# Linear attention with a mixture-of-depths expert on one core: when the expert's weights, the decayed keys and the first batch's slots come in the order of work

## The chip, the cores and the metric

The kernel runs on one core of a Trainium2 chip. The metric is the device time of one execution in microseconds; lower is better. Before the change it is 191.12 us, the median of three runs (190.85 to 191.2).

## What is computed

The inputs are q, k and v with 4 batches, 8 heads, 768 positions and a head dimension of 64, in fp32, and one decay factor per head. The reference first computes a causal linear attention with decay, in blocks of 64 positions:

```python
for b in range(nb):
    intra = (q_b k_b^T * Dmask) v_b              # inside the block, Dmask = lam ** (i - j)
    inter = (q_b * lam_pow) kv_state             # from all blocks before
    out_b = intra + inter
    kv_state = lam_block * kv_state + (k_b * rev_pow)^T v_b
```

The heads are then laid side by side, so that x has 4 batches of 768 rows of 512 values. For each batch a score `x @ w_gate` is computed for every row, the 128 rows with the highest scores are chosen, and for these alone `x + sigmoid(score) * (relu(x @ w1) @ w2)` replaces the row. w1 is 512 x 1024 and w2 is 1024 x 512. All other rows are the attention's output.

## The kernel before, in words

The work is cut into 24 groups of 128 rows (two blocks of 64), six groups to a batch. The loop at L601 goes through the groups; pass g is called step g. Every engine executes its instructions in the order in which the program issues them, so the order of the calls in the loop body is the schedule. The tile framework adds the waits that the data and the buffers need.

Step g does these things for different groups, in this order:

- `load(g + 6)` issues the three input DMAs (q, k, v; 256 KB each, rows of 64 values) on SP's queue, L68. There are seven buffers of each input.
- `load_weights(g - 4)` issues one of eight weight DMAs of 512 KB in steps 4 to 11, on the same queue: four for w1 (L84), four for w2 (L87).
- `decay_state(2g + 4)`, GpSimd (POOL) at L263, multiplies a state by its decay.
- `keys_decayed(g + 3)`, POOL at L183, multiplies the keys by their powers of the decay; it gives kd, which `state_products(g + 3)` needs in the next step.
- `from_scores(g)` (L295) and `outputs(g)` finish group g: TensorE (PE) multiplies, ScalarE (ACT) copies the result to x_b (L309, L311) and stores it (L321).
- `scores(g + 1)` (L230), `from_states(g + 1)` (L284) and `masked(g + 1)` (L237, VectorE, DVE) start group g + 1. `from_states` needs qs, the decayed queries.
- `state_products(g + 2)` (L253) multiplies decayed keys and values into pu, two PSUM banks of which there is one set. It can overwrite them only when `next_state` of the group before has read them.
- `transposes(g + 2)` (L195, L206) with ACT's copies to qT and kT (L198, L212), `queries_decayed(g + 2)` (POOL, L217, gives qs), `next_state(2g + 4)` (DVE, L274), `decay_state(2g + 5)`.
- `gate_scores(g)` (DVE, L334) computes the scores of group g. It needs wg_b, the gate weights repeated on all 128 partitions.
- `row(g - 1)` (L357 on PE, L360 on ACT, L363 on DVE), then `next_state(2g + 5)`, then `compare(g - 1)` (L373) count, for each row, how many scores beat it. At the first row group of a batch `row` also zeroes the counters "beaten" on POOL (L352).

When a batch is complete, `plan(b)` spreads its expert over later steps. `ranks` (L409, L414) turns the counts into ranks and a matrix of hits, `tokens` (L425 to L434) turns the hits into row numbers, `fetch` (L448) gathers the rows xs from the output in memory, `gate` (L458 to L473) transposes them and computes the sigmoid, and sixteen pieces do the two matrix products: eight `hidden` pieces (ph, L486) and eight `back` pieces (py, L500), the last of which also adds the residual (L508) and scatters the rows back (L512). The calls that `plan` puts into a step run with `in_order(pieces)`.

For the first batch (b = 0, s = 6) ranks come in step 7, tokens and fetch in step 8, the gate in step 9 behind `state_products(11)`, and the pieces in steps 9 to 14 as 2, 3, 3, 3, 3, 2. For b = 1 (s = 12) ranks, tokens and fetch are all in step 13, and for b = 2 in step 19. The third batch has one piece in each of steps 21 to 23, and the rest at the end together with the fourth batch's expert.

Of the kernel before, what the change touches and what calls it, by code (L numbers as in the profile page):

```python
# [8 lines left out]
FP32 = mybir.dt.float32  # L9
# [8 lines left out]
def kernel(  # L18
# [12 lines left out]
    nc = tc.nc  # L31

    B, H, S, D = q.shape
    HD = H * D
# [3 lines left out]
    C = 64  # L38
    NT = S // L
    NHP = H // 2  # L40
    NDC = HD // 128
    NFC = F // 128
    NGR = (CAP + 127) // 128
    NG = B * NT
# [5 lines left out]
    const = ctx.enter_context(tc.tile_pool(name="const", bufs=1))  # L50
# [4 lines left out]
    ps_o = ctx.enter_context(tc.tile_pool(name="ps_o", bufs=2, space=PSUM))  # L55
# [6 lines left out]
    def load(g):  # L62
        b, c = divmod(g, NT)
        rows = slice(c * L, (c + 1) * L)
        tiles = []
        for name, src in (("qn", q), ("kn", k), ("vn", v)):
            t = ld.tile([128, H, D], FP32, name=name)
            nc.sync.dma_start(out=t[:], in_=src[b, :, rows, :].rearrange("h p d -> p h d"))  # L68
            tiles.append(t)
        loaded[g] = tiles  # L70


    lam_b = const.tile([128, H], FP32, name="lam_b")
    nc.scalar.dma_start(out=lam_b[:], in_=lam.unsqueeze(0).broadcast_to([128, H]))
    for g in range(3):
        load(g)
    wg_b = const.tile([128, HD], FP32, name="wg_b")
    nc.sync.dma_start(out=wg_b[:], in_=moe_w_gate.unsqueeze(0).broadcast_to([128, HD]))
    w1_sb = const.tile([128, NDC, F], FP32, name="w1_sb")
    w2_sb = const.tile([128, NFC, HD], FP32, name="w2_sb")  # L80

    def load_weights(i):
        if i < NDC:
            nc.sync.dma_start(out=w1_sb[:, i, :], in_=moe_w1[i * 128 : (i + 1) * 128, :])  # L84
        else:
            j = 2 * (i - NDC)
            nc.sync.dma_start(  # L87
                out=w2_sb[:, j : j + 2, :],
                in_=moe_w2[j * 128 : (j + 2) * 128, :].rearrange("(c p) e -> p c e", p=128),
            )  # L90
# [12 lines left out]
        out=not_before[:], in_=not_before[:], compare_op=ALU.is_ge, fill=0.0,  # L103
# [13 lines left out]
    if CAP % 128:  # L117
# [4 lines left out]
            out=in_cap[:], in_=in_cap[:], compare_op=ALU.is_gt, fill=0.0,  # L122
# [5 lines left out]
    for hh in range(2):  # L128
        for hp in range(NHP):
            h = 2 * hp + hh  # L130
            nc.vector.tensor_tensor_scan(
                out=mask[:, hh, hp, :], data0=lam_b[:, h : h + 1].broadcast_to([128, C]),
# [12 lines left out]
    for hp in range(NHP):  # L145
        for c in range(2):
            nc.vector.tensor_tensor_scan(
                out=qpow[:, hp, c, :], data0=lam_p[:, hp : hp + 1].broadcast_to([128, C]),
# [27 lines left out]
    def quarters():  # L176
        for hp in range(NHP):
            for hh, c in ((0, 0), (1, 1), (1, 0), (0, 1)):
                yield hp, hh, c

    def keys_decayed(g):
        kd = att.tile([128, H, D], FP32, name="kd")
        nc.gpsimd.tensor_tensor(  # L183
            out=kd[:], in0=loaded[g][1][:],
            in1=kpow[:].rearrange("p a b -> p (a b)").unsqueeze(2).broadcast_to([128, H, D]),
            op=ALU.mult,
        )
        kds[g] = kd
# [35 lines left out]
    def scores(g):  # L224

        qT, kT = qTs.pop(g), kTs.pop(g)
        po = ps_o.tile([128, 2, 2, NHP, C], FP32, name="po")
        pos[g] = po
        for hp, hh, c in quarters():
            nc.tensor.matmul(  # L230
                po[half[c], hh, 1, hp, :], lhsT=kT[half[hh], hp, half[c]],
                rhs=qT[half[hh], hp, half[c]], start=True, stop=True, skip_group_check=True,
            )
# [10 lines left out]
    def start_u(g):  # L244
        us[g] = [ps_u.tile([128, 512], FP32, name=f"pu{c}") for c in range(2)]
# [125 lines left out]
    def count(b, t, cols, op, at):  # L371
        cmp = mod.tile([128, S], BF16, name="cmp")
        nc.vector.tensor_scalar(  # L373
            out=cmp[:, : cols.stop - cols.start], in0=rows_[b][:, cols],
            scalar1=scs[b][:, t : t + 1], scalar2=None, op0=op, op1=ALU.add,
            accum_out=beatens[b][:, t, at : at + 1],
        )

    def count_later(b, groups, last):
        for t in groups:  # L380
            if upto[b][t] < last:
                cols = slice((upto[b][t] + 1) * L, (last + 1) * L)
                count(b, t, cols, ALU.is_gt, last)
                upto[b][t] = last

    def compare(g):
        b, t = divmod(g, NT)
        first = upto[b].pop(NT + t, 0)
        count(b, t, slice(first * L, (t + 1) * L), ALU.is_ge, t)
        if t == NT // 2 - 1 or t == NT - 1 or (b == B - 1 and t == NT - 2):  # L390
            count_later(b, range(t), t)
        elif t == NT - 2:
            count_later(b, range(NT // 3), t)

    def compare_older(g):

        b, t = divmod(g, NT)
        if t > 0:
            count(b, t, slice(0, t * L), ALU.is_ge, 0)
            upto[b][NT + t] = t  # L400
# [119 lines left out]

    gates, later, ranked = {}, {}, {}
    busy_until = [0]

    def put(step, key, piece):
        later.setdefault(step, []).append((key, piece))
# [5 lines left out]
    def plan(b):  # L533
        last = b == B - 1
        s = (b + 1) * NT
        ranks, tokens = places(b)
        if last:

            def last_row():
                compare_older(NG - 1)  # L540
                row(NG - 1, us[NG][1])
                compare(NG - 1)
                ranks()

            put(s, 35, last_row)
            put(s, 85, tokens)
        else:
            ranked[s + 1] = ranks

            where = (s + 1, 25) if b > 0 else (s + 2, 5)  # L550
            put(*where, tokens)
        for i in range(NGR):
            s = max(s, busy_until[0])
            fetch, gate, pieces = expert(b, i)
            if s + 3 >= NG:
                s = max(s, NG)
                put(s, 86, fetch)
                put(s + 1, 0, gate)
                for j, piece in enumerate(pieces):
                    put(s + 2, j, piece)  # L560
                busy_until[0] = s + 3
                continue
            put(s + 1, 26, fetch) if i > 0 or b > 0 else put(s + 2, 6, fetch)
            gates[s + 3] = gate

            whole = s + 9 <= NG
            counts = [2, 3, 3, 3, 3, 2] if whole else [1, 1, 1]
            assert len(pieces) == 16
            where = [(s + 3 + i, 10 * (j + 1)) for i, n in enumerate(counts) for j in range(n)]
            where = [w for w in where if w[0] < NG]  # L570
            where += [(NG, 10 * (j + 1)) for j in range(len(pieces) - len(where))]
            for (step, key), piece in zip(where, pieces):
                put(step, key, piece)
            busy_until[0] = s + 6 if whole else NG
# [3 lines left out]
    queries_decayed(0)  # L578
    keys_decayed(1)
    scores(0)  # L580
    start_u(0)
    state_products(0)
    next_state(0)
# [13 lines left out]
    decay_state(3)  # L597
    next_state(3)

    n_w = NDC + NFC // 2  # L600
    for g in range(NG):  # L601
        if g + AHEAD < NG:
            load(g + AHEAD)
        if 0 <= g - NT + 2 < n_w:
            load_weights(g - NT + 2)
        if g >= 2 * NT and kept:
            store_kept()
        if g + 2 < NG:
            decay_state(2 * g + 4)
        if g + 3 < NG:  # L610
            keys_decayed(g + 3)
        from_scores(g)
        outputs(g)
        if g + 1 < NG:
            scores(g + 1)
            from_states(g + 1)
            masked(g + 1)
        if g in ranked:
            ranked.pop(g)()
        if g % NT == 0 and g > 0 and NGR:  # L620
            compare_older(g - 1)
        if g + 2 <= NG:
            start_u(g + 2)
        if g + 2 < NG:
            state_products(g + 2)
        if g in gates:
            gates.pop(g)()
        if g + 2 < NG:
            transposes(g + 2)
            queries_decayed(g + 2)  # L630
            next_state(2 * g + 4)
            decay_state(2 * g + 5)
        gate_scores(g)
        pieces = later.pop(g, [])

        rows = [r for r in {NG - 2: [g - 1, g], NG - 1: []}.get(g, [g - 1]) if r >= 0 and NGR]
        if g % NT == 0:
            for r in rows:
                row(r)
        else:  # L640
            in_order(pieces)
            for r in rows:
                row(r, us[NG][0] if r == NG - 2 else None)
        if g + 2 < NG:
            next_state(2 * g + 5)
        for r in rows:
            compare(r)
        if g % NT == 0:
            in_order(pieces)
        if g % NT == NT - 1 and NGR:  # L650
            plan(g // NT)
# [35 lines left out]
```

## Time and profile before

| what | value |
|---|---|
| device time, median of three | 191.12 us |
| span of the profiled run | 184.5 us |
| PE busy | 149.4 us, 81% |
| POOL busy | 103.1 us, 56% |
| DVE busy | 110.7 us, 60% |
| ACT busy | 67.5 us, 37% |
| DMA on the input and weight queue | 23.34 MB in 76688 packets |

The page of a profile gives the busy time of each engine, the span in 40 slices with the busy share of each slice in tenths, the chain of waits that ended last, and the groups of instructions that cost most. In a timeline a row has the start, the duration, engine, line, operation, the tile written and the tile read, the number of instructions joined in the row, and in brackets the idle time of the engine before it with what ended the idle. "issue" is an engine's wait for which the profile shows no releaser. PE matmul rows count the records that the profile has; a matmul in fp32 leaves two records.

### The profile page before, as it was taken

Reading aid. Unit: us, or ns where it says so; the run is one execution under the profiler, and the core shown is the slowest. Engines: PE = TensorE matmul, PEld = TensorE weight load, DVE = VectorE, ACT = ScalarE, POOL = GpSimd, SP = SyncE. Lnnn points to the kernel's source line nnn. Section 1 sums busy time; section 2 is a strip of 40 time slices with the busy share of each in tenths; the row PEclk is TensorE's granted clock in tenths of the full one; section 3 lists DMA queues with packets and bytes.
Section 4 is the critical chain, followed back from the end, with each engine's and each line's share of the span. In section 5 each row is a group of like instructions: output and inputs, shape, how many; then the busy total and the mean of one; then the engine's idle time right before and its main releaser. Section 6 shows DMA issues by size and latency. Waiting matters only on the chain.

```text
span 184.5 us, 8089 instructions
## 1 busy us (share of the span) xinstructions
PE 149.4 (81%) x3520; PEld 121.1 (66%) x3520; DVE 110.7 (60%) x357; ACT 67.5 (37%) x185; POOL 103.1 (56%) x110
## 2 busy tenths in 40 slices
PE   0787577877665809999979999999989969989980
PEld 0675555766654709999566699995767869449630
DVE  2942455675998625665985678759967889430010
ACT  2223355553343504555234455453425631111100
POOL 4286878666785953375837866758678400220002
PEclk9999999999999996999999999999999999999996
DMA  4999999999999999999999979911121311011001
GB/s 102 226 221 245 231 242 225 226 228 234 206 221 246 272 292 260 255 226 240 327 349 265 282 210 250 213 47 62 60 62 59 117 57 60 0 57 57 0 0 57
DMA packets 80898, 32.23 MB, mean 175 GB/s; under 512 B 75616, under 2 KB 75616, under 8 KB 80864
## 3 DMA queue, kind: packets, MB, share of 16 engines
q1 hardware_dynamic: 76688, 23.34, 57.1%
q10 hardware_dynamic: 3536, 6.30, 9.4%
q0 software_dynamic: 640, 2.10, 3.4%
q8 instruction: 27, 0.44, 1.1%
q14 instruction: 7, 0.06, 0.1%
HBM read 24.38 MB, written 7.34 MB: 172 GB/s over the span
## 4 chain that ended last, share of the span: by engine, by line
PE 47%; issue 14%; POOL 10%; DMA 9%; DVE 8%; SPq 6%; ACT 4%; POOLq 1%; ACTq 0%; DVEq 0%
PE ph L486 11%; PE py L500 9%; PE tq L195 6%; SPq L68 5%; PE pu L253 5%; POOL qs L217 5%; PE po L284 4%; PE po L295 4%; POOL decayed L263 3%; ACT qT L198 3%; DMA kn<-in_k_dram 3%; PE po L230 3%; DMA xs<-out_dram,tok 3%; PE pu L206 2%; DVE state L274 2%
## 5 line engine op out<-in xcount | busy, mean ns | idle before, releaser
L263 POOL TENSOR_TENSOR decayed<-state,decay 128x256 f32<-128x256 f32 x40 | 36.7, 919 | 15.0 <-DVE state L274 13.2
L217 POOL TENSOR_TENSOR qs<-qT,qpow 128x512 f32<-128x512 f32 x24 | 31.4, 1307 | 24.4 <-ACT qT L198 22.9
L274 DVE TENSOR_TENSOR state<-pu,decayed 128x256 f32<-128x256 f32 x40 | 16.9, 422 | 25.6 <-ACT kT L212 17.1
L486 PE MATMUL ph<-xsT,w_sb 128*128 128x128 f32 x256 | 31.2, 278 | 0.7 <-ACT xsT L462 0.7
L198 ACT COPY qT<-tq 128x512 f32<-128x512 f32 x24 | 14.0, 584 | 45.4 <-PE tq L195 44.2
L486 PEld LDWEIGHTS ph<-xsT,w_sb 128*128 128x128 f32 x256 | 29.8, 193 | 1.2 <-ACT xsT L462 0.9
L500 PE MATMUL py<-w_sb,hs 128*128 128x512 f32 x64 | 29.7, 600 | 0.4 <-ACT qT L198 0.4
L373 DVE TENSOR_SCALAR_CACHE_REDUCE cmp<-sc_row,sc 128x128 bf16<-128x128 f32 (+3 forms) x66 | 29.9, 497 | 0.0
L183 POOL TENSOR_TENSOR kd<-kn,kpow 128x512 f32<-128x512 f32 x24 | 26.0, 1084 | 4.9 <-DVE kpow L137 3.3
L334 DVE CUSTOM_DVE_ANT_0 xg<-x_b,wg_b 128x512 f32<-128x512 f32 x24 | 25.6, 1066 | 0.0
L284 PE MATMUL po<-state,qs 64*64 64x64 f32 x704 | 18.4, 222 | 8.0 <-issue 4.3
L253 PE MATMUL pu<-vn,kd 64*64 64x64 f32 x704 | 19.3, 225 | 3.8 <-DVE state L274 3.7
L230 PE MATMUL po<-qT,kT 64*64 64x64 f32 x768 | 18.0, 226 | 4.5 <-issue 3.9
L284 PEld LDWEIGHTS po<-state,qs 64*64 64x64 f32 x704 | 14.9, 134 | 10.1 <-issue 5.2
L195 PE MATMUL tq<-ident,qn 128*128 128x128 f32 x96 | 16.9, 303 | 5.1 <-DMA qn<-in_q_dram 5.1
L253 PEld LDWEIGHTS pu<-vn,kd 64*64 64x64 f32 x704 | 16.2, 138 | 4.8 <-DVE state L274 4.5
L230 PEld LDWEIGHTS po<-qT,kT 64*64 64x64 f32 x768 | 14.9, 138 | 5.5 <-issue 4.5
L500 PEld LDWEIGHTS py<-w_sb,hs 128*128 128x128 f32 x64 | 11.3, 190 | 10.9 <-issue 9.8
L295 PEld LDWEIGHTS po<-vn,p 64*64 64x64 f32 x768 | 13.4, 134 | 6.8 <-issue 3.2
L311 ACT COPY x_b<-po 64x256 f32<-64x256 f32 x48 | 17.6, 367 | 0.6
L237 DVE TENSOR_TENSOR p<-po,mask 128x512 f32<-128x512 f32 x24 | 16.5, 686 | 1.8 <-PE po L284 1.7
L295 PE MATMUL po<-vn,p 64*64 64x64 f32 x768 | 16.7, 224 | 0.9 <-DVE p L237 0.9
(61 smaller groups left out, 148.1 us busy)
## 6 DMA issues: line engine op xcount, KB each, us to landing
qn<-in_q_dram SPq DMA_DIRECT2D x24, 256.0 KB, 5.6
kn<-in_k_dram SPq DMA_DIRECT2D x24, 256.0 KB, 5.9
vn<-in_v_dram SPq DMA_DIRECT2D x24, 256.0 KB, 5.8
out_dram<-x_b ACTq DMA_DIRECT2D x18, 256.0 KB, 3.3
w_sb<-in_moe_w_dram SPq DMA_DIRECT2D x8, 512.0 KB, 5.5
out_dram<-x_b ACTq DMA_DIRECT2D x2, 768.0 KB, 7.4
wg_b<-in_moe_w_gate_dram SPq DMA_DIRECT2D x1, 256.0 KB, 6.1
xs<-out_dram,tok POOLq DMA_INDIRECT x4, 4.4
```

The lines of the kernel that those rows point to most:

```text
L183: nc.gpsimd.tensor_tensor(out=kd[:], in0=loaded[g][1][:], in1=kpow[:].rearrange("p a b -> p (a b)").unsqueeze(2).broadcast_to([128, H, D]) ...
L195: nc.tensor.transpose(tq[:, hp, :], in_=loaded[g][0][:, 2 * hp : 2 * hp + 2, :], identity=ident[:])
L217: nc.gpsimd.tensor_tensor(out=qs[:], in0=qTs[g][:], in1=qpow[:].rearrange("p a c i -> p a (c i)"), op=ALU.mult)
L230: nc.tensor.matmul(po[half[c], hh, 1, hp, :], lhsT=kT[half[hh], hp, half[c]], rhs=qT[half[hh], hp, half[c]], start=True, stop=True, skip_g ...
L253: nc.tensor.matmul(us[g][c][half[hh], hp * D : (hp + 1) * D], lhsT=kd[half[c], h, :], rhs=vn[half[c], h, :], start=True, stop=True, skip_g ...
L263: nc.gpsimd.tensor_tensor(out=t[:], in0=states[n][:], in1=decay[:], op=ALU.mult)
L284: nc.tensor.matmul(pos[g][half[hh ^ c], hh, 0, hp, :], lhsT=qs[half[hh], hp, half[c]], rhs=states[n][half[hh], hp, :], start=(hp == 0), st ...
L295: nc.tensor.matmul(pos[g][half[hh ^ c], hh, 0, hp, :], lhsT=p[half[c], hh, hp, :], rhs=vn[half[c], 2 * hp + hh, :], start=(hp == 0 and (2 ...
L334: nc.vector.tensor_tensor_reduce(out=xg[:], in0=x_bs[b][:, t].rearrange("p a b e -> p (a b e)"), in1=wg_b[:], scale=1.0, scalar=0.0, op0=A ...
L373: nc.vector.tensor_scalar(out=cmp[:, : cols.stop - cols.start], in0=rows_[b][:, cols], scalar1=scs[b][:, t : t + 1], scalar2=None, op0=op, ...
L486: nc.tensor.matmul(ph[:, fc % 4, :], lhsT=w1_sb[:, dc, fc * 128 : (fc + 1) * 128], rhs=keep["xsT"][:, dc, :], start=(dc == 0), stop=(dc == ...
L500: nc.tensor.matmul(py[:], lhsT=keep["hs"][:, fc, :], rhs=w2_sb[:, fc, :], start=(fc == 0), stop=(fc == NFC - 1),)
```

## The change

The change has six parts, all in the order of the work; what is computed is the same.

1. The gate weights are no longer loaded as a 256 KB broadcast. One row of 2 KB is loaded on ACT's queue, and a matmul with a column of ones behind `scores(0)` spreads it over the partitions; ACT copies the result to wg_b.
2. The four w1 DMAs are issued together in step 2, behind the inputs of group 8, and the four w2 DMAs in steps 4 to 7.
3. `keys_decayed(g + 3)` moves from the start of the step to behind `decay_state(2g + 5)` and `gate_scores(g)`, ahead of the pieces and rows of the step; in step 7 alone it stands behind the comparisons, and so behind the fetch.
4. The first batch's ranks are computed at the end of step 6, its tokens and its fetch come in step 7, and its gate at the end of step 8.
5. The first batch's sixteen pieces are done in steps 9 to 12, four in each.
6. The third batch has one piece in step 21, two in step 22 and none in step 23.

The purpose is to have the first batch's rows gathered before PE needs them, and the weights on the chip by then, without holding up POOL by keys that have not landed.

The diff's core:

```diff
+wg_row = const.tile([1, HD], FP32, name="wg_row")
+nc.scalar.dma_start(out=wg_row[:], in_=moe_w_gate.unsqueeze(0))
...
+ones = const.tile([1, 128], FP32, name="ones")
+nc.vector.memset(ones[:], 1.0)
 wg_b = const.tile([128, HD], FP32, name="wg_b")
-nc.sync.dma_start(out=wg_b[:], in_=moe_w_gate.unsqueeze(0).broadcast_to([128, HD]))
...
-            ranked[s + 1] = ranks
-            where = (s + 1, 25) if b > 0 else (s + 2, 5)
-            put(*where, tokens)
+            ranked[s + 1 if b > 0 else s] = ranks
+            put(s + 1, 25, tokens)
...
-            put(s + 1, 26, fetch) if i > 0 or b > 0 else put(s + 2, 6, fetch)
-            gates[s + 3] = gate
+            put(s + 1, 26, fetch)
+            first = b == 0 and i == 0
+            if first:
+                late_gates[s + 2] = gate
+            else:
+                gates[s + 3] = gate
...
-            counts = [2, 3, 3, 3, 3, 2] if whole else [1, 1, 1]
+            counts = [1, 2] if not whole else [4, 4, 4, 4] if first else [2, 3, 3, 3, 3, 2]
...
     scores(0)
+    po = ps_o.tile([128, 2, 2, NHP, C], FP32, name="po")
+    po = po[:, 0].rearrange("p a b i -> p (a b i)")
+    nc.tensor.matmul(po, lhsT=ones[:], rhs=wg_row[:], start=True, stop=True)
+    nc.scalar.copy(out=wg_b[:], in_=po)
...
-    n_w = NDC + NFC // 2
+    weights_at = [NT // 2 - 1] * NDC + [NT // 2 + 1 + i for i in range(NFC // 2)]
     for g in range(NG):
         if g + AHEAD < NG:
             load(g + AHEAD)
-        if 0 <= g - NT + 2 < n_w:
-            load_weights(g - NT + 2)
+        for i, at in enumerate(weights_at):
+            if at == g:
+                load_weights(i)
...
-        if g + 3 < NG:
-            keys_decayed(g + 3)
         from_scores(g)
...
-        if g in ranked:
+        if g in ranked and g % NT:
             ranked.pop(g)()
...
         rows = [r for r in {NG - 2: [g - 1, g], NG - 1: []}.get(g, [g - 1]) if r >= 0 and NGR]
+        fetched = g == NT + 1
+        if g + 3 < NG and not fetched:
+            keys_decayed(g + 3)
...
         for r in rows:
             compare(r)
+        if g + 3 < NG and fetched:
+            keys_decayed(g + 3)
+        if g in ranked:
+            ranked.pop(g)()
+        if g in late_gates:
+            late_gates.pop(g)()
```

## The prediction

> **What bounds the kernel now.** I read the page's slices first, then the chain, then the timeline of single steps. "Step g" is pass g of the loop at L601; "start of step g" is the first L295 matmul. Busy time and slices of the page:
>
> ```profile
> PE 149.4 (81%) x3520; PEld 121.1 (66%) x3520; DVE 110.7 (60%) x357; ACT 67.5 (37%) x185; POOL 103.1 (56%) x110
> ...
> PE   0787577877665809999979999999989969989980
> ...
> DMA  4999999999999999999999979911121311011001
> ```
>
> PE is three quarters busy up to slice 14 (65 us), has a hole there, and is then nearly full. DMA is full for 110 us. So there are two regimes, and the hole between them. The chain in order of time names the hole, and the table of windows its after-effect (columns: window, length, busy PE, PEld, DVE, ACT, POOL, clock, DMA share, GB/s):
>
> ```profile
> 62.96 1.18 POOL decayed L263
> 64.14 0.17 issue
> 64.32 4.84 DMA xs<-out_dram,tok
> 69.16 0.14 issue
> 69.30 1.09 PE pt L458 x4
> ```
>
> ```profile
> 62.00:69.30 7.30, 2.23 (x114) 2.04 (x113) 3.56 (x12) 1.48 (x5) 5.02 (x5) 0.97 1.15 279
> 69.30:74.00 4.70, 4.70 (x29) 4.60 (x29) 2.43 (x7) 1.86 (x5) 2.01 (x2) 0.68 1.14 260
> ```
>
> PE stands 5.1 us for the gather of the first batch's slots, then runs at clock 0.68: four tq transposes take 1.06 us where they take 0.66 elsewhere; with pt, tq, tk and ph that is about 1.4 us. The hole costs 6.5 us.
>
> In the first regime no engine is full; a loop of waits is. Timeline, end of step 1:
>
> ```profile
> 24.38 1.27 POOL L217 TENSOR_TENSOR qs<-qT,qpow 128x512 f32<-128x512 f32 x1 [0.27 <-ACT qT L198]
> ...
> 25.61 1.18 POOL L263 TENSOR_TENSOR decayed<-state,decay 128x256 f32<-128x256 f32 x1
> ...
> 26.73 0.13 POOL L352 MEMSET beaten<- 128x42 f32 x1
> ...
> 26.89 0.35 DVE L363 SCALAR_TENSOR_TENSOR cmp<-pb,sc,not_before 128x128 bf16<-128x128 f32 x1 [0.69 <-POOL beaten L352]
> ...
> 27.17 0.42 DVE L274 TENSOR_TENSOR state<-pu,decayed 128x256 f32<-128x256 f32 x1
> ...
> 27.64 0.69 PE L253 MATMUL pu<-vn,kd 64*64 64x64 f32 x30 [0.52 <-DVE state L274]
> ```
>
> A round is pu to tq 0.62, to qT 0.75, to qs 0.67, to decayed 1.24, decayed 1.18, state 0.45, pu again 0.05: 4.95 us. Measured from pu to pu in steps 1 to 7: 5.3, 5.1, 4.5, 5.7, 5.2, 5.0, 6.5; the rest is PE "issue" gaps of 0.4 to 2.1 us. kd(g+3) runs before qs, in the 2 us in which POOL waits for qT anyway; POOL still idles 0.2 to 0.5 us there, so kd is free today. In the second regime PE work between tq and the next pu (some 2.2 us plus the expert's pieces) is longer than the POOL leg of 4 us: a step with three pieces takes 5.8 to 6.2 us.
>
> **What the skill says.** The Trainium skill, "SBUF — State Buffer", Who interferes with whom: a vector operation with two SBUF inputs and a GpSimd one that reads SBUF block each other. The trace agrees: decayed takes 0.73 us alone, 1.18 beside xg, and xg 0.68 or 1.18. "TensorE: Matmul & The Clock Gate", Part 1: an idle array falls to half clock; agrees with the 0.68 after the hole. "Runtime: NRT & Kernel Launch", Instruction fetch mechanics: instructions come in 16 KiB blocks by a DMA queue, "mostly hidden". The trace has the blocks (q8: 27 packets, 0.44 MB), but with full DMA engines I read the issue gaps as fetches not hidden; that differs. "DMA: Bandwidth & Descriptors", Specifications: under 512 B a descriptor misses line rate; agrees: 231 to 240 GB/s in windows of 256-byte rows alone, up to 331 with larger rows.
>
> **The change, part by part.**
>
> *Gate row.* The 256 KB broadcast leaves SP's queue (1.31 us of issue, about 1 us of DMA). A 128x512 matmul and a 128x512 ACT copy come in behind scores(0). The matmul is not in the trace: two records of 0.43 us as in py, up to double on the cold clock of the first 10 us: 0.9 to 1.7 us. ACT's copy (0.6) lies in an ACT idle of 2.85. Behind the matmul waits pu(0), then state and decayed(1); POOL was not free for decayed(1) before 11.30, and state was done at 10.24, so 1.06 us is hidden. Added: 0 to 0.9, taken 0.5. The new po tile also makes scores(1) wait for x_b(0); pu(2) waits for state until 16.72, which hides it.
>
> *kd last.* In step g kd now follows decayed(2g+5). pu(g+3) needs kd(g+3), and stands in the next step: the round becomes decayed end, kd 1.04, pu 0.08 in place of state 0.45 and 0.05, that is 5.5 us. Behind pu stand tq, qT and qs, the loop itself. Steps 2, 5 and 6: 5.5 against 5.1, 5.2, 5.0, +1.2 at most, 0 if the issue gaps do not overlap; taken 0.9. Steps 3 and 4 have no decayed(11) or an issue gap as long: 0. In step 0 kd waited for kn until 18.34 and delayed qs by 0.7; pu(3) waits for kd again, so it gains nothing.
>
> *kd before the zeroing.* In steps 1, 13 and 19 row() zeroes "beaten" on POOL, and DVE's cmp and state queue behind. kd now precedes it (in 13 and 19 also the gather): 1.05 us more before state, whose wait by PE ended last in step 1 (above) and in step 19 (0.48 us at 137.43). Step 1: 1.0. Step 19: 1.0. Step 20: 5.5 against 4.9, +0.6. Step 13 is below.
>
> *Slots a step earlier.* ranks (0.2) and hit (1.0 to 1.5) now precede p(8) and the pk matmuls of step 7: PE waits for hit, and gather (1.15) and zeroing stand before cmp, state and kd(10). From pu(9): hit 2.5, p 3.2, state and decayed 4.9, tok 5.3, gather 6.5, kd 7.65, pu(10) 7.7; before 6.5: +1.2. Then tq, tk, pb until 9.5; the rows land at 5.3+4.84=10.15, so pt waits only 0.7. Step 9 starts at 10.8; pu(11) 12.9, tq and tk to 14.5, four pieces of 0.9, step 10 at 18.35. From pu(10) 10.65, against 14.37 before (59.70 to 74.07): -3.7. The hole goes, but two more pieces are done in this stretch.
>
> *Four by four.* A step with three ph pieces takes 5.9, so with four 6.8, with four py 6.9 to 7.0: steps 10 to 12 take 20.7, before 18.1: +2.6. Steps 13 and 14 lose their five pieces, but are then held by POOL: in step 13 qs, decayed, kd, gather, zeroing, cmp, state give pu(16) 9.1 us after the step's start (before 9.07), then a round of 5.5 (before 5.84): -0.3.
>
> *Weights.* w1 (2 MB) passes ahead of group 9: at 240 to 330 GB/s, 6.4 to 8.7 us, less 1 for the broadcast. kn(9) was issued by 41.7 and lands some 5.9 later; now about 51 to 54. kd(9) is due near 54.5, and later groups have 2 us or more. Nothing, on the edge.
>
> *Last expert.* One ph piece moves from step 23 to 22, into PE's idle of 1.44 before 150.06. The end hangs on DVE (busy without a break from 150.7 to 157.3), tok and the gather, not on that piece: 0.
>
> Sum: 0.5+1.0+0.9+1.2-3.7+2.6-0.3+1.6 = +3.8 us: 191.12+3.8 = 194.9.
>
> **Rivals.** *Faster: the hole wins.* The new waits fall into the issue gaps: start 0.3, step 1 0.5, rounds 0, step 7 0, stretch to step 10 -3.7, four-piece steps +1.6, steps 13 and 14 -0.9, steps 19 and 20 +0.5: -1.7, 189.4. For it: gaps of up to 2.1 us, and a hole of 6.5. Against: in step 1 and step 19 PE waits for state and no gap. *Slower still: inputs late.* The margin at kd(9) is 0 to 3 us and pu(9) needs vn(9), issued after kn(9); 2.5 us of waiting gives 197.4. For: DMA shares of 0.92 to 1.15 over steps 6 to 9. Against: the compute itself is later by 2.4 us there. *No change*: parts cancel, 191.1.
>
> **Numbers.** Likeliest 0.60; hole wins 0.22; inputs late 0.13; no change 0.05. Range 189.3 to 197.6: both rivals' values are inside, and about 2 in 10 beyond them or beyond the bounds of start and rounds. Faster 0.24 (the rival and a little of the main case), same 0.05, slower 0.71.
>
> **What would show it.** Right: no wait of PE on xs above 1 us and no clock dip near 70; pu L256 waiting for POOL kd in steps 2 to 7; DVE cmp waiting 1.7 us for beaten in step 1; steps 9 to 12 near 6.8 us with PE full; POOL-bound rounds in 13 and 14. Wrong: pu never waits for kd (kd-last is free), or steps 13 and 14 near 5 us each (hole wins), or kd and tq waiting for kn, qn of groups 9 to 12 (inputs late).

## The result and the profile after

The changed kernel takes 199.82 us (198.54 to 200.43) where the kernel before took 190.99 us (189.91 to 191.2) on the same chip: 1.0466 times as long, 95% interval 1.040 to 1.0531. The prediction was 194.9 us in a range of 189.3 to 197.6. The direction was right and the size was not: +8.8 us where I had summed +3.8.

The times of one kernel differ by up to four per cent from execution to execution and from chip to chip, so below each kernel is compared by its ratio to the kernel before, measured beside it on the same chip; the bracket behind a ratio is its 95% interval, and a difference of ratios is turned into us with some 189 us, the time of the kernel before. The ratios take only the fast executions of both kernels, so they differ a little from the quotient of the medians that are given beside them. A profile is one execution: that of before ran in 186.2 us and that of after in 200.0, so these two lie further apart than the medians. "Step g" is, as above, pass g of the loop and starts with its first from_scores matmul.

Of the page of after, the totals and three of the slices (a slice is 5 us):

```profile
PE 157.3 (79%) x3522; PEld 126.6 (64%) x3522; DVE 111.8 (56%) x358; ACT 68.3 (34%) x186; POOL 105.1 (53%) x110
...
PE   0896688775776089999998288999996997999990
...
PEclk9999976998799958999999879999999999999999
DMA  5999999996999999994589989411013211011001
```

PE still has a hole in slice 14, a second one in slice 23, and its clock, full up to slice 15 (69 us) before, is now low in slices 6, 7, 10, 11, 15 and 16 and again in 23 and 24. The waits, as total us, times and longest:

```profile
PE pu L256 <- POOL kd L186: 15.5, 11, 5.3
...
DVE cmp L366 <- POOL beaten L355: 12.3, 4, 4.7
...
POOL xs L451 <- issue: 4.0, 3, 3.0
```

The first is new: before, PE never waited for kd. The second was 4.7 us in all. Of PE's wait for the gathered rows, 5.07 us before, nothing is left. The chain in order of time shows what stands at 65 us in its place:

```profile
63.63 1.19 POOL decayed L266
64.82 2.81 issue
67.62 0.02 POOLq L186
67.64 0.17 issue
67.81 1.14 POOL xs L451
...
69.11 1.01 POOL kd L186
70.12 0.04 issue
70.17 1.23 PE pu L256 x24
```

The hole has changed its owner. The slots are ready at 64.49 (DVE's cast to tok), but POOL starts the gather at 67.81, and kd(10) and pu(10) stand behind it: PE waits 5.34 us. The end of step 1 in the timeline, the counterpart of the one shown before:

```profile
27.97 1.19 POOL L266 TENSOR_TENSOR decayed<-state,decay 128x256 f32<-128x256 f32 x1
...
29.12 1.04 POOL L186 TENSOR_TENSOR kd<-kn,kpow 128x512 f32<-128x512 f32 x1
...
30.10 0.13 POOL L355 MEMSET beaten<- 128x42 f32 x1
...
30.21 0.33 PE L256 MATMUL pu<-vn,kd 64*64 64x64 f32 x2 [1.31 <-POOL kd L186]
30.26 0.35 DVE L366 SCALAR_TENSOR_TENSOR cmp<-pb,sc,not_before 128x128 bf16<-128x128 f32 x1 [1.69 <-POOL beaten L355]
...
30.54 0.42 DVE L277 TENSOR_TENSOR state<-pu,decayed 128x256 f32<-128x256 f32 x1
```

kd lies between decayed and the zeroing; PE waits for kd and DVE for the zeroing, 1.69 us where I had written 1.7. And the windows (length, busy PE, PEld, DVE, ACT, POOL, clock, DMA share, GB/s) of step 2, of one undisturbed round, and of steps 8 and 14:

```profile
27.00:34.20 7.20, 5.41 (x142) 4.69 (x141) 3.09 (x9) 2.47 (x8) 4.24 (x6) 0.74 1.07 241
...
54.42:59.91 5.49, 3.71 (x137) 3.20 (x137) 5.15 (x20) 2.32 (x7) 4.09 (x5) 1.00 1.11 255
63.20:74.30 11.10, 5.76 (x143) 5.11 (x143) 3.62 (x13) 2.61 (x8) 5.69 (x7) 0.74 1.09 268
...
107.00:116.50 9.50, 5.58 (x138) 4.70 (x137) 3.57 (x11) 2.24 (x7) 5.64 (x8) 0.82 1.05 270
```

The round from 54.42 to 59.91 is exactly my 5.5 us, at full clock. Step 2 takes 7.2 at a clock of 0.74. Counted by the starts of the steps, after is 2.05 us behind before at step 0, 4.8 at step 3, 7.5 at step 8, 12.3 at step 9, back at 7.6 at step 14, and 13.8 at step 23. From there to the end both take 34.2 us.

### The profile page after: what moved, and what is told of

It is laid out like the page before. It is cut to its first block, busy times and chain, and to the rows that moved or that the text cites. A ratio compares the mean times of both kernels' runs of the same rounds, so it can differ in the third digit from the quotient of the medians.

```text
span 198.3 us, 8102 instructions
## 1 busy us (share of the span) xinstructions
PE 157.3 (79%) x3522; PEld 126.6 (64%) x3522; DVE 111.8 (56%) x358; ACT 68.3 (34%) x186; POOL 105.1 (53%) x110
## 4 chain that ended last, share of the span: by engine, by line
PE 44%; POOL 21%; issue 15%; DVE 7%; DMA 6%; ACT 4%; POOLq 1%; ACTq 0%; DVEq 0%
PE ph L489 8%; PE tq L198 8%; PE pu L256 8%; POOL decayed L266 7%; PE py L503 7%; POOL kd L186 6%; POOL qs L220 6%; DMA out_dram<-y,tok 4%; ACT qT L201 4%; DVE cmp L376 3%; PE po L233 3%; PE po L298 3%; PE po L287 3%; DMA qn<-in_q_dram 2%; PE pu L209 2%
## 5 line engine op out<-in xcount | busy, mean ns | idle before, releaser
L266 POOL TENSOR_TENSOR decayed<-state,decay 128x256 f32<-128x256 f32 x40 | 38.8, 969 | 8.1 <-DVE state L277 6.8
L256 PE MATMUL pu<-vn,kd 64*64 64x64 f32 x704 | 20.7, 244 | 19.9 <-POOL kd L186 15.5
L337 DVE CUSTOM_DVE_ANT_0 xg<-x_b,wg_b 128x512 f32<-128x512 f32 x24 | 27.0, 1123 | 0.0
L198 PE MATMUL tq<-ident,qn 128*128 128x128 f32 x96 | 18.8, 327 | 4.7 <-DMA qn<-in_q_dram 4.7
L287 PE MATMUL po<-state,qs 64*64 64x64 f32 x704 | 16.6, 221 | 3.6 <-issue 2.6
L366 DVE SCALAR_TENSOR_TENSOR cmp<-pb,sc,not_before 128x128 bf16<-128x128 f32 x22 | 7.6, 345 | 20.7 <-POOL beaten L355 12.3
L233 PE MATMUL po<-qT,kT 64*64 64x64 f32 x768 | 17.0, 225 | 2.7 <-issue 2.3
L298 PEld LDWEIGHTS po<-vn,p 64*64 64x64 f32 x768 | 14.3, 143 | 7.0 <-issue 3.8
L298 PE MATMUL po<-vn,p 64*64 64x64 f32 x768 | 17.7, 233 | 0.5 <-DVE p L240 0.3
L287 PEld LDWEIGHTS po<-state,qs 64*64 64x64 f32 x704 | 14.0, 136 | 4.8 <-issue 3.2
```

The costliest lines, as they stand in the source:

```text
L198: nc.tensor.transpose(tq[:, hp, :], in_=loaded[g][0][:, 2 * hp : 2 * hp + 2, :], identity=ident[:])
L233: nc.tensor.matmul(po[half[c], hh, 1, hp, :], lhsT=kT[half[hh], hp, half[c]], rhs=qT[half[hh], hp, half[c]], start=True, stop=True, skip_g ...
L256: nc.tensor.matmul(us[g][c][half[hh], hp * D : (hp + 1) * D], lhsT=kd[half[c], h, :], rhs=vn[half[c], h, :], start=True, stop=True, skip_g ...
L266: nc.gpsimd.tensor_tensor(out=t[:], in0=states[n][:], in1=decay[:], op=ALU.mult)
L287: nc.tensor.matmul(pos[g][half[hh ^ c], hh, 0, hp, :], lhsT=qs[half[hh], hp, half[c]], rhs=states[n][half[hh], hp, :], start=(hp == 0), st ...
L298: nc.tensor.matmul(pos[g][half[hh ^ c], hh, 0, hp, :], lhsT=p[half[c], hh, hp, :], rhs=vn[half[c], 2 * hp + hh, :], start=(hp == 0 and (2 ...
```

## The experiments

My theory after the comparison was that keys last costs most of it, in every round and twice: by the wait, and by the low clock that the waits leave behind. The rivals were the 2 MB of w1 in one burst, the start, and the packing four by four. I went from both ends: one part undone in the changed kernel, and one part alone in the kernel before.

### Keys first again, and keys last alone

The first run is the changed kernel with this back at the head of the step:

```diff
+        if g + 3 < NG:
+            keys_decayed(g + 3)
         from_scores(g)
...
-        if g + 3 < NG and not fetched:
-            keys_decayed(g + 3)
```

> The changed kernel with one part undone: keys_decayed(g+3) stands again ahead of from_scores in every step. Theory 'keys last' (pu waits 1.3 to 1.4 us for kd in each early step, 5.3 in step 7, and these waits also lower the granted clock to 0.74-0.80, so they cost twice): most of the 8.8 us goes, 191 to 194, granted clock 0.97 or more, PE waits on kd near zero. Rival 'burst' (the 2 MB of w1 ahead of group 9 delay stores and inputs, and kd only shows it): 198 to 200, the wait moves from kd to kn or to state. Rival 'start and four by four': 198 to 200 with the early steps shorter and the loss again in steps 9 to 13.

193.26 us against 188.32, ratio 1.0197 (1.009 to 1.0304): some 5.1 us of the 8.8 come back. The second is the kernel before with the opposite edit and nothing else:

> The kernel before with this part alone: keys_decayed(g+3) stands behind the second decayed product in every step, and nothing else is changed. Theory 'keys last': slower by 5 to 8 us (196 to 199), with waits of PE on kd of 1.3 us in steps 2 to 6 and a clock of 0.75 to 0.85 there. Rivals 'burst' and 'start and four by four': 191 to 193, since neither the weights nor the pieces nor the start are touched; the recorded sum gives +0.9 for steps 2, 5, 6, +1.0 for step 1 and +1.6 for steps 19 and 20, so 194.6 if my terms were rightly sized.

196.47 us, ratio 1.0382 (1.0294 to 1.0471): 7.2 us for this part alone. Its waits have the line "PE pu L253 <- POOL kd L183" with 10.5 us, 11 times, longest 1.4. The chain of this run shows the round, once cold and once warm:

```profile
29.58 0.87 PE pu L253 x30
30.45 1.06 PE tq L195 x4
...
31.58 0.59 ACT qT L198
...
32.25 0.78 POOL qs L217
33.03 0.45 issue
33.48 1.18 POOL decayed L263
34.66 1.01 POOL kd L183
35.67 0.04 issue
35.71 0.68 PE pu L253 x16
36.39 0.60 PE tq L195 x4
```

kd has taken the place of the state in the loop, and PE waits for it in every step from 2 to 9. In this profile step 9, which holds the hole, takes 15.2 us where it took 12.1 in that of before: the rows were 6.0 us on their way instead of 4.8, and the clock was low for 10 us instead of 3.4. The rivals fall as main causes: burst, packing and start are not in this kernel. The first run lacks keys last and is still 3.7 us slower than before, so there is a second part.

### Early or late

To see which rounds pay, keys last was applied to half of the steps of the kernel before (g < NT + 3, or g >= NT + 3):

> The kernel before with keys last in steps 0 to 8 alone, keys first from step 9 on. My recorded terms for these steps are +1.0 (step 1) and +0.9 (steps 2, 5, 6), that is 1.010. If the early rounds carry the missing part, since every round waits for kd and not only three: 1.02 to 1.03 (4 to 5.5 us). If the missing part is in the later steps: 1.01 or less.

> The kernel before with keys last from step 9 on alone (keys first in steps 0 to 8). Keys last in all steps gave 1.0382. If the early rounds carry most of it: 1.01 or less, about my terms for steps 19 and 20 (1.6 us, 0.8 per cent). If the later steps carry as much as the early ones: 1.02 or more, with waits of PE on kd or state in steps 13 to 21.

Steps 0 to 8 alone: 1.0182 (1.0104 to 1.026), 3.4 us where my terms said 1.9. From step 9 on: 1.0148 (0.9981 to 1.0316), 2.8 us where they said 1.6, but with an interval that reaches down to nothing. Together 6.2 of the 7.2 us. The early rounds cost more than I gave them, though the lower end of the interval (2.0 us) lies close to my 1.9; for the later ones the run can't tell 1.6 from 2.8.

### The low clock

In the kernel before with keys last, matmuls that add zeros to po were put on PE between from_states and pu, where it waits for kd, in steps 0 to 4, 6 and 7. NHP is 4, so these are sixteen; with range(1) in place of range(2) they are eight:

```diff
             from_states(g + 1)
+            if g < NT + 2 and g != NT - 1:
+                for _ in range(2):
+                    for hp in range(NHP):
+                        for hh in range(2):
+                            nc.tensor.matmul(
+                                pos[g + 1][half[0], hh, 0, hp, :], lhsT=ident[half[hh], :C],
+                                rhs=zero[half[hh], :], start=False, stop=False, skip_group_check=True,
+                            )
             masked(g + 1)
```

> The kernel before with keys last, and in steps 0 to 4, 6 and 7 sixteen extra 64x64 matmuls that add zeros to po, standing on PE between from_states and pu, where it waits for kd. They add work to PE and take nothing else away. If the waits cost by themselves only (my recorded round of 5.5 us): 196 to 197 or a little more. If they cost by the clock (pu and tq at 1.1 instead of 0.7 us, both in the loop): the clock of steps 2 to 8 comes back to 0.95 or more and 2.5 to 4 us of the 7 to 8 are regained, 192 to 194.5.

> The kernel before with keys last in all steps, and eight extra 64x64 matmuls that add zeros to po in PE's wait for kd (sixteen gave 1.055 where none gave 1.0382, and took up to 1.0 us of a wait of 1.2 to 1.4). Theory 'low clock': the clock of steps 2 to 8 rises and the rounds with pu and tq at 1.06 to 1.10 us go to 5.5: 1.02 to 1.03. Theory 'the waits alone': 1.038 or more.

Sixteen: 1.055 (1.0495 to 1.0604), slower than without them; they take 1.03 us, and in step 3, behind an issue gap of 0.84 us, they came on top of it. Eight: 1.0382 (1.0211 to 1.0553), the same as without them. With eight the clock did rise early: of the first 60 us, slices 7 and 10 to 12 are low without them and slice 10 alone with them. The clock lines of the two pages, first of keys last alone:

```profile
PEclk9999996998887975699999999999999999999998
```

and with eight matmuls:

```profile
PEclk9999999996997585699999999999999999999999
```

In this profile step 8 starts at 57.3 where it started at 60.4 without them. But step 8, in which none of the eight stand, then ran on a low clock from 61.3 us on and took 8.9 us instead of 6.3, and step 10 starts at 82.4 and 81.9: the gather was issued 0.8 us earlier (69.2 and 70.0) and landed no earlier (pt at 76.53 and 76.21). Over the whole profile the mean granted clock is 0.945 with the eight and 0.943 without: the low stretches were moved and not removed. So these runs don't decide whether the low clock costs anything beyond the waits. That it costs twice, as my theory had it, is not shown, and not refuted either. With sixteen the mean clock was 0.971, but they bring work of their own.

### The slots, the packing, the row and the weights, one after the other

Three kernels between before and the first run above: slots alone, then the packing, then the gate row as well (keys first in all):

> The kernel before with one part alone: the slots of the first batch found a step earlier (ranks and hit at the end of step 6, the tokens, the gather and the first gate in steps 7 and 8), pieces 2,3,3,3,3,2, broadcast, weights and keys first as before. My recorded terms: step 7 +1.2 and the hole's -3.7, with no piece shifted: 1.5 to 2.5 us faster than before if they were rightly sized. Rival 'POOL chain of step 7' (hit, tokens, gather and zeroing stand ahead of the state of step 7 and of qs in step 8, whatever the place of kd): no gain or up to 2 us slower, with a PE wait of over 2 us on state or hit in steps 6 to 8.

> The kernel before with the slots a step earlier and the four steps of four pieces; broadcast, weights and keys first as before. The recorded term for the packing is +2.6 in steps 10 to 12 and -0.3 in 13 and 14, so 2.3 us above the run with the slots alone. If the pieces only change places (16 of them in either case, and PE full in both), it is within 0.5 us of it. w1 is complete only by about step 9 here, so a wait of ph on w1 in step 9 is possible and would speak for the burst's purpose.

> The changed kernel with keys first and the weights spread as before: slots, four by four and the gate row. Theory 'burst holds up instruction fetches and stores' (with keys first and the burst, the profile has a PE issue gap of 3.9 us at 43 and a wait of 5 us on qn near 60): 189.5 to 191 here against 193 with the burst. Rival 'the burst is neutral' (with keys last the weights made no difference): 192 to 194. Gate row: 0.5 to 2 us above the run without it.

Slots alone: 187.75 us against 189.13, ratio 0.9881 (0.9804 to 0.9957), 2.2 us faster. The packing on top: 1.0155 (1.008 to 1.0229), that is +5.2 us. The terms 1.2 - 3.7 and 2.3 can't be set beside these two runs as they stand; the account of the prediction below says why. In the trace of the run with the packing the hole is not gone. The chain at the gather, and PE's row behind it:

```profile
59.74 7.57 DMA xs<-out_dram,tok
...
67.45 0.63 PE L458 MATMUL pt<-ident,xs 128*128 128x128 f32 x4 [3.71 <-DMA xs<-out_dram,tok]
```

The rows were 7.57 us on their way where the kernel before took 4.84, and PE waited 3.71 us for them. In all seven kernels with early slots and keys first it was 5.7 to 7.6 us; PE's wait for the rows was 4.05 us at most, and in two of the seven there was none. The row on top of both: 1.0192 (1.0123 to 1.0262), +0.7. Then the weights: 1.0197 in the first run, +0.1; the burst is neutral in time. In the trace of that run PE stands for 3.9 us beside it, with no releaser that the profile shows:

```profile
46.84 0.48 PE L233 MATMUL po<-qT,kT 64*64 64x64 f32 x5 [3.93 <-issue]
```

With the weights spread such gaps are more and shorter, and no less in sum (9.1 us in gaps of over 0.5 us, against 8.5).

Two more undo a part in the changed kernel, the weights (weights_at = [NT - 2 + i ...]) and the row:

> The changed kernel with the weights spread as before (one piece of w1 in each of steps 4 to 7, of w2 in 8 to 11), all else kept. Theory 'keys last': 198 to 200, the same waits on kd. But step 9 of the changed kernel needs w1 at once (its first pieces stand in step 9), and w1 is then complete only near 65 us, still in time. Rival 'burst': 193 to 195, PE's waits of step 7 and the store of 48 us gone.

> The changed kernel with the gate row fetched by the 256 KB broadcast again, without the 128x512 matmul (2.07 us on the profile) and its copy. Theory 'keys last': 198 to 199.8, at most the 0.5 us of my sum. Rival 'start': step 0 begins 2.05 us later than before in the profile, so 197.5 to 198 with all of it returned; if the cold clock of the first steps hangs on it, 196.

Weights spread: 1.0558 (1.0454 to 1.0662), if anything worse than 1.0466. Row as before: 1.0374 (1.0269 to 1.0479), 1.7 us better. Both intervals overlap that of the changed kernel.

### POOL's 3 us ahead of the gather

The 2.81 us of "issue" in the chain had no releaser: the slots were there, and the last store of the batch had been issued 22 us earlier (45.93). The six kernels with keys last and early slots that were run without this test all have such a gap (2.11 to 3.00 us; in four of them the profile names the landing of an input of a later group as its end, which the gather has no use for), none with keys first has it (0.16 to 0.18). An 8 KB packet of the instruction queue q14 starts at 65.3, inside the gap. In all six such a packet starts within the gap or at most 0.2 us before it, and POOL goes on 1.5 to 2.0 us after the packet has ended. The test adds eight POOL instructions where POOL waits anyway:

```diff
             transposes(g + 2)
+            if g == 4:
+                pad = mod.tile([128, 8], FP32, name="pad")
+                for i in range(8):
+                    nc.gpsimd.memset(pad[:, i : i + 1], 0.0)
             queries_decayed(g + 2)
```

> The changed kernel with eight memsets of a 128x1 scratch tile on POOL ahead of qs(6) in step 4, where POOL waits 2 us for qT anyway. In the changed kernel POOL stands idle 3.00 us ahead of the gather of step 7 (67.81) though its slots are ready at 64.49, and an instruction packet of 8 KB moves at 65.25 to 65.5, inside that time. Theory 'POOL waits for its own next block of instructions': eight more instructions make the block end earlier, ahead of a qs that waits anyway; the idle time ahead of the gather falls under 0.5 us, PE's wait on kd in step 7 from 5.3 to 2 to 3 us, and the time by 1 to 3 us (ratio 1.02 to 1.04). Rival 'it waits for a transfer or for PE' (order unchanged): the 3 us stay, ratio 1.046.

The timeline of POOL in that run:

```profile
64.67 1.18 POOL L266 TENSOR_TENSOR decayed<-state,decay 128x256 f32<-128x256 f32 x1
66.02 1.14 POOL L451 DMA_INDIRECT xs<-out_dram,tok  x1 [0.17 <-DMA kn<-in_k_dram]
```

The idle time ahead of the gather is 0.17 us, PE's wait on kd in step 7 fell from 5.34 to 2.58, and the third of these packets now moves between 54 and 56 us, 11 us ahead of the gather. Nothing but the number of POOL instructions ahead of this point was changed, and gap and packet moved as expected: I take the gap for POOL waiting for its next instructions, on one profile of the test. What POOL does in the 1.5 to 2.0 us after the packet is not shown. In the time it is 1.0396 (1.030 to 1.0493), some 1.3 us, which the intervals don't hold apart from none.

### The zeroing, and the pieces

The changed kernel with the zeroing of beaten moved from row() to the end of the step in which the batch begins, and the changed kernel with pieces 2,3,3,3,3,2:

> The changed kernel with the zeroing of beaten emitted at the end of the step in which the batch begins (steps 0, 6, 12, 18), so that it no longer stands behind kd in steps 1, 7, 13 and 19. My recorded terms say +1.0 for step 1 and +1.0 for step 19, so 1 to 2 us should come back (ratio about 1.037), with DVE's cmp no longer waiting for POOL in steps 1 and 19 and PE's wait on state at 151 gone. Rival 'kd itself is the last wait there': within 0.5 us of the changed kernel.

> The changed kernel with the first expert's pieces 2,3,3,3,3,2 over six steps again. With keys first, the packing cost 2.7 per cent (1.0155 against 0.9881) where I had reckoned 1.2 per cent (2.3 us). If that is the packing itself: ratio 1.02 to 1.03. If it came in e6 from the gather's wait and the low clock behind it, which keys last has already in another form (wait on kd in step 7): 1.03 to 1.046.

Zeroing earlier: 1.0348 (1.0248 to 1.0448), 2.2 us better, near the 2.0 of my two terms, with an interval that overlaps that of the changed kernel. Step 19 in the timeline of after,

```profile
150.05 0.15 POOL L355 MEMSET beaten<- 128x42 f32 x1
150.24 0.35 DVE L366 SCALAR_TENSOR_TENSOR cmp<-pb,sc,not_before 128x128 bf16<-128x128 f32 x1 [2.67 <-POOL beaten L355]
...
150.98 0.69 PE L256 MATMUL pu<-vn,kd 64*64 64x64 f32 x30 [1.50 <-DVE state L277]
```

and of this run, where cmp waits 0.60 for ACT and PE for nothing:

```profile
143.72 0.35 DVE L364 SCALAR_TENSOR_TENSOR cmp<-pb,sc,not_before 128x128 bf16<-128x128 f32 x1 [0.60 <-ACT sc_row L361]
...
144.75 0.92 PE L256 MATMUL pu<-vn,kd 64*64 64x64 f32 x32
```

Pieces as before: 1.0342 (1.0268 to 1.0417), 2.3 us better; the intervals just overlap. The windows of steps 12, 13 and 14 of that run:

```profile
90.40:96.70 6.30, 6.12 (x144) 4.11 (x143) 5.16 (x18) 3.17 (x9) 4.42 (x6) 1.00 0.77 254
96.70:102.70 6.00, 6.00 (x150) 4.12 (x149) 5.75 (x21) 2.24 (x6) 3.94 (x4) 1.00 1.18 258
102.70:109.40 6.70, 5.22 (x145) 3.80 (x144) 2.71 (x8) 2.51 (x7) 4.46 (x7) 1.00 1.06 259
```

Steps 13 and 14 hold five pieces here and take 12.7 us; in the changed kernel they hold none and take 4.5 + 9.5 = 14.0. Steps 9 to 12 take 24.2 here and 28.2 there. The two profiles thus put some 5.3 us on the packing, more than the times do.

### The place of the scatter

A reason why steps 13 and 14 give nothing back offered itself. With four by four the last piece stands in step 12, so y's scatter stands on POOL ahead of decayed, qs and the next gather:

```profile
104.68 1.03 POOL L515 DMA_INDIRECT out_dram<-y,tok  x1 [2.40 <-DVE y L511]
105.75 1.41 POOL L266 TENSOR_TENSOR decayed<-state,decay 128x256 f32<-128x256 f32 x1
...
111.34 1.00 POOL L451 DMA_INDIRECT xs<-out_dram,tok  x1 [0.79 <-issue]
```

The scatter's own transfer holds up little: it landed 5.9 us after its start, at 110.54, when POOL was just done with kd (110.55). Both runs move one piece of sixteen, and the scatter with it, to step 14:

```diff
-            counts = ... [4, 4, 4, 4] if first ...
+            counts = ... [4, 4, 4, 3, 0, 1] if first ...
```

> The changed kernel with the first expert's pieces 4,4,4,3,0,1: one matmul of 16 pieces, and with it y and the scatter, goes from step 12 to step 14. If the scatter's place on POOL is what the packing costs: the 2.4 us of POOL's wait for y and the wait of the gather for the scatter go, steps 13 and 14 together fall from 14.0 to about 11.5, and the ratio from 1.0466 to 1.030 to 1.037. If PE's packing itself costs: within 0.5 per cent of 1.0466.

> The same piece moved in the run with keys first (slots and four by four; broadcast and weights as before: 1.0155). If the scatter's place is the cause: 0.995 to 1.005, within my own term of the run with the slots alone (0.9881). If not: 1.012 to 1.018.

1.051 (1.0415 to 1.0605) and 1.0144 (1.0044 to 1.0244): no gain that the time shows in either. In the trace of the first the wait for y is gone from POOL (the scatter is at 116.76, idle 0.17), the gather starts 0.16 us after kd, and steps 13 and 14 still take 5.8 + 8.1 = 13.9 us: PE waits there for hit (0.69), for pb behind tok_f (1.45) and for the state (1.12). In the trace of the second, with keys first, they take 5.8 + 4.9 = 10.7 us, where they took 13.3 with that piece in step 12. So the scatter's place is not shown to be what the packing costs; with keys first the trace speaks for it, and the time doesn't show it, though its interval just reaches the 1.005 that the expectation asked for.

The trace of the run with the zeroing earlier says more of these two steps. In the changed kernel the zeroing for the third batch stands on POOL behind the scatter, both decayed products, qs, kd and the gather. DVE's cmp waits for it, the state stands behind cmp, and PE waits for the state:

```profile
112.53 0.35 DVE L366 SCALAR_TENSOR_TENSOR cmp<-pb,sc,not_before 128x128 bf16<-128x128 f32 x1 [3.29 <-POOL beaten L355]
...
113.37 1.13 PE L256 MATMUL pu<-vn,kd 64*64 64x64 f32 x30 [2.44 <-DVE state L277]
```

With the zeroing a step earlier both waits are gone, and steps 13 and 14, pieces and scatter as in the changed kernel, take 4.5 + 5.4 = 9.9 us (columns as above):

```profile
101.05:105.54 4.49, 3.51 (x145) 3.09 (x144) 4.00 (x10) 2.24 (x6) 2.32 (x2) 1.00 1.22 238
105.54:110.97 5.43, 3.97 (x139) 3.38 (x138) 3.57 (x11) 1.76 (x5) 4.75 (x6) 1.00 1.14 304
```

These 4.1 us are more than the trace shows for the steps that my two terms name (1.2 us in steps 1 and 2, 1.5 in 19 and 20). That the 2.2 us of the time came so near to the 2.0 of the terms is therefore in part luck.

### Versions that beat both kernels

The slots alone do (0.9881). Two attempts to add to them, the early zeroing, and with it the gate at its old place in step 9:

> A candidate: the kernel before with the slots a step earlier (ratio 0.9881) and the zeroing of beaten at the end of steps 0, 6, 12, 18; keys first, pieces, weights and broadcast as before. Theory: cmp and state no longer wait for POOL in steps 1, 7, 13, 19 (6.5 us of DVE waits in the run with keys first), some 1 to 2 us on PE's path: 0.975 to 0.985. Rival: the waits of those steps lie beside PE's issue gaps: 0.985 to 0.99.

> A candidate: the kernel before with the slots a step earlier, the zeroing a step earlier, and the first expert's gate at its old place in step 9, two steps after its gather, so that PE waits neither for the gather nor for a late gate; keys first, pieces, weights and broadcast as before. In the run with slots and zeroing alone PE still waited 4.05 us for the gather on the profile, so 1 to 3 us come back: 0.975 to 0.985. Rival: that wait is POOL's and PE's issue gap in another form, 0.985 to 0.99.

186.08 us against 188.90, ratio 0.9883 (0.9842 to 0.9924): faster than both kernels, and no better than the slots alone. With keys first the zeroing costs nothing that the time shows. With the gate later: 0.9859 (0.9655 to 1.0064); PE's wait for the gathered rows falls to 0.59 us and one of 1.46 us for w1 comes in its place.

## Why the prediction was wrong in size, step by step

The direction was right, and most of the waits that I named are in the traces. Two terms were too small: the stretch from step 7 to step 10, where I let the hole go, and keys last, which I charged to three rounds.

*Start, +0.5.* The matmul left two records that end 2.07 us after its start at 8.50, above my upper bound of 1.7, and ACT's copy came at once after it. The 0.43 us in the prediction is the distance between two py records; each lasts 0.59, so two of them take 1.02 us, and here they took twice that. Measured 0.7 (added) and 1.7 (undone), neither clear of noise. Perhaps a little short.

*Keys last, +0.9 for steps 2, 5 and 6, with +1.0 for step 1 and +1.6 for steps 19 and 20: 3.5 in all.* This term failed from whichever side it is measured: 5.1 (undone) and 7.2 (alone). The mechanism was right: kd for state in the loop, a round of 5.5 us, the zeroing behind kd; the trace shows each of them. The size was not, because I charged the 5.5 only to three steps and let "the issue gaps overlap" cancel much of it. The waits are in all steps from 2 to 9 (10.5 us of waiting, 11 times), and steps 0 to 8 alone cost 3.4 us where I had 1.9. Of the terms inside, that for the zeroing is near what was measured (2.0 said, 2.2 measured in the changed kernel), though the trace puts most of it in steps 13 and 14.

*Slots a step earlier, +1.2 and -3.7, and four by four, +2.6 and -0.3.* My -3.7 has four pieces in step 9, two of which came there by the packing, at 0.9 us each. Like for like, I had said -4.3 for the slots alone (1.2 - 3.7 - 1.8) and +4.1 for the packing (2.3 + 1.8), together -0.2. Measured with keys first: -2.2 (-3.7 to -0.8) and +5.2, together +2.9 (1.5 to 4.3). In the changed kernel the packing cost 2.3. The sum of the two is thus 3.1 us off, and this is the larger of the two failures.

The step of it that failed is "The hole goes". With four pieces in step 9 I had the stretch from step 7 to step 10 shorter by 2.5 us. In the ten traces of such kernels it is between 1.5 us shorter and 3.0 us longer than in that of before, and 0.95 longer in the run with slots and packing alone. I took the gather's 4.84 us over from before, and a wait of 0.7 behind it; with keys first the rows were up to 7.57 us on their way, and PE waited up to 4.05. In the changed kernel it is POOL that comes late: pu(10) comes 10.26 us after pu(9) (70.17 and 59.91) where I had 7.7, and 2.8 of it is POOL's gap ahead of the gather, most likely a wait for instructions, which I had looked for on PE alone. There is a clock dip near 70 as before, where I had named its absence as a sign of being right. Why the gather takes longer when it is issued earlier stays open.

The four-piece steps were right (6.7, 6.7 and 7.1), and steps 13 and 14 right in kind: POOL holds them, through gather, zeroing, cmp and state, as I had written, and they take 1.3 us more than before where I had 0.3 less. How the 5.2 divides between the step 9, the steps 10 to 12 and this chain is not shown.

*Weights, "nothing, on the edge".* Right: +0.1 added, no gain undone. No engine that computes waits for kn, vn or qn of groups 9 to 12.

*Last expert, 0.* Right: 34.2 us from step 23 to the end in both.

*The rivals.* "The hole wins" did not come: the slots alone gain 2.2 us, and the rest of the change loses more. "Inputs late" did not come. The measured terms, in the order in which they were added, are -2.2 + 5.2 + 0.7 + 0.1 + 5.1 = 8.9; they are steps of one chain of kernels, so they give the 8.8 of the result by construction, up to rounding. Slots and packing (2.9 for -0.2) and keys last (5.1 for 3.5) hold 4.7 of the 5.0 us that were missing.

## What to carry to other kernels

When an operation is moved to the end of an in-order queue, look for who reads it first after the move: if that reader opens the loop that sets the pace, charge the difference to every round of that loop, and don't let gaps seen elsewhere pay for it. Place an operation that is free in a wait (here kd in POOL's wait for qT) only where there is still a wait. When two terms of a sum move the same work, write down which of them holds it, or neither can be checked by a run of its own. Look for every reader of a late operation, the small ones too: here a zeroing of 0.14 us behind a gather held up two steps. And when an idle time has no releaser, pad the queue and look whether it moves: here eight instructions took nearly 3 us of idle time away from the place ahead of the gather.

## What the runs showed of the hardware

An engine other than PE stood still, most likely for its instructions: POOL 2.11 to 3.00 us in six kernels, with a DMA share of 1.09 around it in the changed one, and eight more instructions ahead moved the gap away. The Trainium skill, "Runtime: NRT & Kernel Launch", Instruction fetch mechanics, calls the crossing of a block "mostly hidden"; if the gaps are such crossings, they were not hidden here, with the DMA engines full.

Short waits were enough for a low clock. The longest wait of PE in step 2 of the changed kernel is 1.31 us, and the clock of that window is 0.74; pu and tq take 1.10 and 1.06 us at it where they take 0.69 and 0.60. The table of the Trainium skill, "TensorE: Matmul & The Clock Gate", Part 1, has the clock fall after an idle window of about 3.4 us; here it fell without one. What it followed in these traces is the busy share of PE. The clock was granted in stretches of 3.4 us, full or half. Over the 20 traces, a full stretch was followed by a half one in 55 of 55 cases where PE had been busy for less than 1.4 us of it, in 30 of 48 cases between 1.4 and 1.9 us, and in 1 of 837 above that. Eight small matmuls per wait held the clock up to 60 us but for one slice; it was low later instead, and neither the mean clock of the profile nor the time changed.
